# A delta-rule and soft-MoE kernel: the instruction order of its attention part written by hand instead of by the scheduler

## The chip, the cores and the metric

The kernel runs on one core of one Trainium2 chip. The metric is device microseconds of one execution. A core has TensorE (PE, with its weight loads shown apart as PEld), VectorE (DVE), ScalarE (ACT), GpSimd (POOL) and the DMA queue of SyncE (SP). Each engine runs its own instructions in the order in which they were emitted; engines wait for each other by semaphores.

## The reference

A delta-rule attention runs over 768 tokens for 4 batches of 8 heads with 48 numbers a head; its output, as 3072 rows of 384, goes through a soft mixture of experts with 8 experts of 4 slots.

```python
k_n = k / (np.linalg.norm(k, axis=-1, keepdims=True) + 1e-06)
for t in range(S):
    y[:, :, t] = q_t @ state
    state += beta_t * outer(k_t, v_t - k_t @ state)
logits = x @ phi
d = softmax(logits, axis=0); slot_input = d.T @ x
slot_out[e] = relu(slot_input[e] @ w1[e]) @ w2[e]
out = softmax(logits, axis=1) @ slot_out
```

## The kernel before

The attention is cut into 24 chunks of 32 tokens, numbered 0 to 23 (`x` or `cc` in the code), and six groups of four chunks (`n`; `c` is the place of a chunk in its group, 0 to 3). All 32 heads are worked on together. The state of a chunk is the next chunk's input, so the chunks make one chain. A chunk's chain (function `chunk`) has these links, in this order:

- psR: 16 products of the old state with the keys on PE (L278, into psR), and as many with the queries (into psY)
- R: values minus psR, on DVE (L283)
- psW: 32 small products of R with the inverse of the group (TT) on PE (L289), copied to U by ACT (L292)
- psS: 32 products that update the state on PE (L299), copied out by ACT for one half (L311) and then by DVE for the other (L309), both called S
- outputs: 32 products into psY (L316), copied to Y by ACT (L318). They are not needed by the next chunk.

Beside the chain runs work for later and earlier chunks:

- Preparation (`prep`) of the chunk eight places ahead: two times four transposes of K and Q (L173, copied to KQ by ACT, L176), then 32 products (L188), whose two halves ACT copies to Lc (L194) and DVE to AT (L195). The PSUM tile pt, of which there are two, serves all of this and the routing.
- The inverse (`invert`) of the next group, mainly on DVE: `spread` (L207) and `norms` (L221 to L233, with one square root on ACT, L222), a scaling on POOL (lb, L230), then 31 steps of an elimination, each a product (pr, L240) and a subtraction (tt, L243) that follow each other, then a scaling on POOL (L247) and a transpose into TT (L253). The group's first solve needs TT.
- Scaling of V two chunks ahead on POOL (L259).
- Routing (`route`) of the group that was finished last: four turns of Y (L336), logits (L345), a transpose to lg (L351, L352), softmax over slots (L356 to L364), a running maximum (L370 to L385), weights d (L389), a repeat of d by PE (L398), and four slot products (L410) added to sacc on DVE.

Loads of K and Q run twelve chunks ahead on the SP queue, loads of V six.

What sets the order: the Python code emits a chunk's chain with calls of `fill()` in three places and at the end, and each call emits a share of a merged list of preparation, inverse and routing steps. The scheduler of the framework then orders the instructions of each engine by its own estimates; the code's order is only one of its inputs. Chunks -8 to -1 emit preparation and the first inverse alone. After chunk 23 the last routing is drained, the attention's memory is given up, the weights of the remaining experts are loaded, and the experts and the output run (L489 to L600). That last part is called the tail here.

Of the kernel before, what the change touches and what calls it, by code (L numbers as in the profile page):

```python
# [16 lines left out]
def kernel(  # L17
# [23 lines left out]
    nc = tc.nc  # L41
# [225 lines left out]
    def chunk(cc, Yn, fill):  # L267
# [5 lines left out]
        pr = ps.tile([P, B, G, D], F32, name="psR", tag="psRW")  # L273
        py = ps.tile([P, B, G, D], F32, name="psY", tag="psY")
        for a, dst in enumerate((pr, py)):
# [5 lines left out]
            if a == 0:  # L281
                R = wk.tile([P, U, D], F32, name="R", tag="R")
                nc.vector.tensor_tensor(R, Vt.pop(cc), pr.rearrange("p b g d -> p (b g) d"),  # L283
                                        op=ALU.subtract)
        fill()
        pw = ps.tile([P, U, D], F32, name="psW", tag="psRW")
        for u in range(U):
            for h in range(4):
                nc.tensor.matmul(pw[hs[h], u], lhsT=T[hs[h], u], rhs=R[hs[h], u],  # L289
                                 start=(u == 0), stop=True, skip_group_check=True)  # L290
        Ut = wk.tile([P, U, D], F32, name="U", tag="U")
        nc.scalar.activation(Ut, pw, ACT.Copy)  # L292
        fill()

        if cc < NCH - 1:
            for b in range(B):
                for g in range(G):
                    for h in range(4):
                        nc.tensor.matmul(psS[DP * g:DP * g + D, h, b * D:(b + 1) * D],  # L299
                                         lhsT=K[hs[h], b * G + g, 0:D],  # L300
                                         rhs=Ut[hs[h], b * G + g],
# [10 lines left out]
            fill()  # L312
        for b in range(B):
            for g in range(G):
                for h in range(4):
                    nc.tensor.matmul(py[hs[h], b, g], lhsT=at[hs[h], g, b], rhs=Ut[hs[h], b * G + g],  # L316
                                     start=False, stop=True, skip_group_check=True)
        nc.scalar.activation(Yn[:, c, :, 0:GD], py.rearrange("p b g d -> p b (g d)"), ACT.Copy)  # L318
# [7 lines left out]
    def route(n, Yn):  # L326
# [13 lines left out]
        def logits():  # L340
# [7 lines left out]
            lT = wk.tile([P, P], F32, name="lT", tag="lT", bufs=1)  # L348
            nc.scalar.activation(lT, pl, ACT.Copy)
            pq = pt([P, P])  # L350
            nc.tensor.transpose(pq, lT, ident)  # L351
            nc.vector.tensor_copy(lg.rearrange("p b s -> p (b s)"), pq)  # L352

        def over_slots():
            mx = small.tile([P, B], F32, name="mx", tag="mx")
            nc.vector.tensor_reduce(mx, lg, axis=AX.X, op=ALU.max)  # L356
            el = small.tile([P, B, NSL], F32, name="el", tag="el")
            nc.vector.tensor_tensor(el, lg, mx.unsqueeze(2).broadcast_to([P, B, NSL]),
                                    op=ALU.subtract)
            nc.scalar.activation(el, el, ACT.Exp)  # L360
            nc.vector.tensor_reduce(mx, el, axis=AX.X, op=ALU.add)
            nc.vector.tensor_scalar(mx, mx, 1e-9, None, op0=ALU.add)
            nc.vector.reciprocal(mx, mx)
            nc.gpsimd.tensor_tensor(Call[:, n], el, mx.unsqueeze(2).broadcast_to([P, B, NSL]),  # L364
                                    op=ALU.mult)

        def maximum():

            cm = small.tile([P, 4, NSL], F32, name="cm", tag="cm")
# [3 lines left out]
                                  cm[:, 0, :].unsqueeze(1).broadcast_to([P, 3, NSL]))  # L373
            pm = pt([P, P])
# [3 lines left out]
            else:  # L378
# [6 lines left out]
                nc.vector.tensor_copy(mrun, m1)  # L385
            pmb = pt([P, NSL])
# [33 lines left out]
        return ([lambda b=b: turn(b) for b in range(B)] + [logits, over_slots, maximum, repeat]  # L420
# [7 lines left out]
    NF = 4  # L428

    class Fill:  # L430


        def __init__(self, steps):
            self.steps, self.at, self.calls = steps, 0, 0

        def __call__(self, last=False):
            self.calls += 1
            to = len(self.steps) if last else len(self.steps) * min(self.calls, NF) // NF
            while self.at < to:
                self.at += 1  # L440
                self.steps[self.at - 1]()

    def merge(*lists):

        keyed = [((i + 0.5) / len(ls), j, f) for j, ls in enumerate(lists) for i, f in enumerate(ls)]
        return [f for _, _, f in sorted(keyed, key=lambda x: x[:2])]

# [5 lines left out]
    def quarter(ls, c):  # L453
        return ls[len(ls) * c // GC:len(ls) * (c + 1) // GC]

    routing, inv = [], []
    for x in range(-LEAD, NCH):
# [6 lines left out]
        if 1 <= n + 2 and x == -4:  # L464
            for e in range(NW1):
                load_w1(e, wpool, NW1)
        if c == 0:
            inv = invert(n + 1) if 0 <= n + 1 < NG else []
# [4 lines left out]
        if x < 0:  # L473
# [155 lines left out]
```

## Time and profile before

| what | us |
|---|---|
| median of 3 runs | 491.54 |
| lowest, highest | 484.33, 493.37 |
| the profiled execution, whole | 491.42 |
| its span, first to last instruction | 489.7 |

The span is the time that all rows below count in; the profiled execution is 1.72 us longer than it. A row of the timeline names a start, a duration, an engine, a line, an operation, the tile written, the tiles read, and in brackets how long the engine had been idle and who ended that. A row of the chain names a start, a duration and a piece of work that the end waited for. A row of the waits names the waiting engine, tile and line, whom it waited for, the sum, the count and the longest. A row of the windows gives, for a stretch, the busy time of each engine with its number of instructions, and the mean clock granted to TensorE (1.00 is 2.4 GHz, 0.50 is 1.2 GHz).

### The profile page before, as it was taken

The numbers are of one execution on the slowest core, as the hardware profiler recorded it, in microseconds if no ns is written. First come the engines' busy times: TensorE is split into PE (matmuls) and PEld (weight loads), VectorE is DVE, ScalarE is ACT, GpSimd is POOL, SyncE is SP. The second block draws the span as 40 slices with busy tenths as digits, with TensorE's granted clock in tenths as the row PEclk, the third lists the DMA queues.
The fourth block names the chain that finished last, engine by engine and source line by source line (L and its number), as shares of the span: only waits on it lengthen the run. The fifth ranks groups of instructions, "written<-read, shape, count | busy, mean of one in ns | idle before, by whom it ended". The sixth has DMA issues, their size and how long they took to land.

```text
span 489.7 us, 20564 instructions
## 1 busy us (share of the span) xinstructions
PE 334.7 (68%) x9387; PEld 248.3 (51%) x9387; DVE 245.1 (50%) x679; ACT 128.9 (26%) x257; POOL 63.6 (13%) x88
## 2 busy tenths in 40 slices
PE   5743374656766758788677776876875865788586
PEld 4532263545645646666466655665664753532133
DVE  4159716972168942379721788325997212210033
ACT  2331122121322422332422233224312222111012
POOL 9210112012020040020210200202301000000000
PEclk9655556665766759755778577599798797799695
DMA  6557742320322213202221110010300029949427
GB/s 114 86 94 195 205 83 51 52 37 18 52 51 39 46 19 52 50 16 40 51 39 33 19 19 13 9 20 5 113 23 1 4 94 367 424 156 434 208 101 287
DMA packets 84759, 45.53 MB, mean 93 GB/s; under 512 B 79392, under 2 KB 82624, under 8 KB 82624
## 3 DMA queue, kind: packets, MB, share of 16 engines
q1 hardware_dynamic: 81920, 43.67, 32.4%
q8 instruction: 74, 1.21, 1.0%
q10 hardware_dynamic: 2176, 0.39, 0.4%
q0 software_dynamic: 576, 0.15, 0.3%
q14 instruction: 13, 0.11, 0.1%
HBM read 39.47 MB, written 4.72 MB: 90 GB/s over the span
## 4 chain that ended last, share of the span: by engine, by line
DVE 27%; issue 25%; PE 19%; SPq 10%; DMA 10%; POOL 5%; ACT 3%; DVEq 0%; POOLq 0%; ACTq 0%
DVE pr L240 9%; SPq L80 9%; DVE tt L243 9%; DMA w2t<-in_moe_w_dram 4%; PE pso L567 3%; DVE S L309 3%; PE psR L278 2%; PE pt L410 2%; DMA w1t<-in_moe_w_dram 2%; PE psY L278 2%; POOL lb L230 2%; DMA Q<-in_q_dram 2%; DVE TT L253 2%; PE ph L543 1%; DMA out_dram<-ob 1%
## 5 line engine op out<-in xcount | busy, mean ns | idle before, releaser
L240 DVE TENSOR_TENSOR pr<-tt,lb 128x31 f32<-128x31 f32 (+15 forms) x186 | 68.0, 365 | 17.7 <-POOL lb L230 12.2
L243 DVE TENSOR_TENSOR tt<-tt,pr 128x31 f32<-128x31 f32 (+15 forms) x186 | 66.3, 357 | 5.7
L289 PE MATMUL psW<-R,TT 32*32 32x48 f32 x1536 | 29.9, 242 | 47.0 <-DVE R L283 45.5
L173 PE MATMUL pt<-ident,K 128*128 128x128 f32 x96 | 36.0, 396 | 24.1 <-DVE AT L195 18.7
L289 PEld LDWEIGHTS psW<-R,TT 32*32 32x32 f32 x1536 | 25.7, 134 | 52.4 <-DVE R L283 49.3
L176 ACT ACTIVATE KQ<-pt 128x512 f32<-128x512 f32 x48 | 27.1, 595 | 73.9 <-PE pt L173 73.5
L278 PE MATMUL psR<-S,KQ 128*32 128x96 f32 x768 | 33.1, 324 | 17.7 <-DVE S L309 17.0
L316 PE MATMUL psY<-U,AT 32*32 32x48 f32 x1536 | 39.0, 256 | 3.2 <-issue 3.1
L195 DVE TENSOR_TENSOR AT<-pt,tri 128x128 f32<-128x128 f32 x48 | 11.9, 288 | 54.6 <-ACT Lc L194 54.4
L188 PE MATMUL pt<-KQ 48*32 48x64 f32 x1536 | 33.5, 246 | 6.2 <-ACT KQ L176 2.6
L309 DVE COPY S<-psS 48x768 f32<-48x768 f32 x23 | 22.1, 961 | 31.1 <-ACT S L311 30.7
L316 PEld LDWEIGHTS psY<-U,AT 32*32 32x32 f32 x1536 | 31.1, 143 | 9.2 <-issue 7.1
L299 PE MATMUL psS<-U,K 32*48 32x48 f32 x1472 | 25.3, 261 | 14.5 <-ACT U L292 11.6
L278 PEld LDWEIGHTS psR<-S,KQ 128*32 128x32 f32 x768 | 23.7, 145 | 22.4 <-DVE S L309 18.9
L188 PEld LDWEIGHTS pt<-KQ 48*32 48x32 f32 x1536 | 25.0, 119 | 16.0 <-ACT KQ L176 9.5
L173 PEld LDWEIGHTS pt<-ident,K 128*128 128x128 f32 x96 | 17.3, 186 | 30.7 <-DVE AT L195 20.2
L278 PE MATMUL psY<-S,KQ 128*32 128x96 f32 x768 | 32.3, 314 | 0.0
L292 ACT ACTIVATE U<-psW 128x384 f32<-128x384 f32 x24 | 11.8, 490 | 75.6 <-PE psW L289 75.6
L299 PEld LDWEIGHTS psS<-U,K 32*48 32x48 f32 x1472 | 20.4, 155 | 20.7 <-ACT U L292 15.7
L410 PE MATMUL pt<-Y,dr 32*32 32x97 f32 x768 | 25.1, 271 | 8.5 <-DVE AT L195 4.3
L230 POOL TENSOR_TENSOR lb<-lb,gm 128x1024 f32<-128x1024 f32 x6 | 11.5, 1911 | 141.0 <-DVE gm L229 141.0
L173 PE MATMUL pt<-ident,Q 128*128 128x128 f32 x96 | 29.7, 364 | 0.0
(124 smaller groups left out, 454.9 us busy)
## 6 DMA issues: line engine op xcount, KB each, us to landing
w1t<-in_moe_w_dram SPq DMA_DIRECT2D x8, 1536.0 KB, 8.2
w2t<-in_moe_w_dram SPq DMA_DIRECT2D x8, 1536.0 KB, 15.1
K<-in_k_dram SPq DMA_DIRECT2D x96, 48.0 KB, 2.3
V<-in_v_dram SPq DMA_DIRECT2D x96, 48.0 KB, 2.3
out_dram<-ob SPq DMA_DIRECT2D x24, 192.0 KB, 2.3
Q<-in_q_dram SPq DMA_DIRECT2D x88, 48.0 KB, 2.3
Q<-in_q_dram ACTq DMA_DIRECT2D x8, 48.0 KB, 3.0
bb<-in_beta_dram POOLq DMA_DIRECT2D x16, 6.0 KB, 3.0
```

What stands on the lines that cost most here:

```text
L80: eng.dma_start(out=dst[C * h:C * h + C, :, 0:D], in_=src.rearrange("b (g h) s d -> h s (b g) d", h=4)[h, cc * C:(cc + 1) * C])
L173: nc.tensor.transpose(tp[:, i, a, :], src[:, b * G:(b + 1) * G, :].rearrange("p g d -> p (g d)"), ident)
L176: nc.scalar.activation(KQ[cc][:, 2 * bh:2 * bh + 2], tp, ACT.Copy)
L188: nc.tensor.matmul(pg[g][rh, b], lhsT=KQ[cc][r, b, 0, rh], rhs=KQ[cc][r, b, :, rh], start=True, stop=True, skip_group_check=True)
L240: nc.vector.tensor_tensor(prv, tt[:, j, 0:m].unsqueeze(1).broadcast_to([P, w, m]), lb[:, j, j + 1:C].unsqueeze(2).broadcast_to([P, w, m]), ...
L243: nc.vector.tensor_tensor(tt[:, j + 1:C, 0:m], tt[:, j + 1:C, 0:m], prv, op=ALU.subtract)
L278: nc.tensor.matmul(dst[hs[h], b].rearrange("p g d -> p (g d)"), lhsT=kq[:, b, a, hs[h]], rhs=old[:, h, b, :], start=(b == 0), stop=False, ...
L289: nc.tensor.matmul(pw[hs[h], u], lhsT=T[hs[h], u], rhs=R[hs[h], u], start=(u == 0), stop=True, skip_group_check=True)
L299: nc.tensor.matmul(psS[DP * g:DP * g + D, h, b * D:(b + 1) * D], lhsT=K[hs[h], b * G + g, 0:D], rhs=Ut[hs[h], b * G + g], start=(cc == 0 a ...
L309: nc.vector.tensor_copy(dst, src)
L316: nc.tensor.matmul(py[hs[h], b, g], lhsT=at[hs[h], g, b], rhs=Ut[hs[h], b * G + g], start=False, stop=True, skip_group_check=True)
L410: nc.tensor.matmul(pa[r], lhsT=st["dr"][r, c, b, :], rhs=Yn[r, c, b, 0:GD + 1], start=(b == 0), stop=(b == B - 1), skip_group_check=True)
```

## The change

The attention part is emitted inside `tc.manual_schedule()`, where each engine gets its instructions in the order of the code. `chunk` now returns its five links as functions, the routing's steps are cut so that each holds one pass from one engine to the next (logits and by_tokens, maxima, over_tokens, shares, weights), and `plan` deals the 31 elimination steps of a group over five places in each of its four chunks. The arithmetic, the tiles, the buffers and the loads are the same. The last routing's drain and the tail stand outside of the hand order.

```diff
-    def chunk(cc, Yn, fill):
+    def chunk(cc, Yn):
...
+        return rest, read, solve, update, outputs
...
-        return ([lambda b=b: turn(b) for b in range(B)] + [logits, over_slots, maximum, repeat]
+        return ([lambda b=b: turn(b) for b in range(B)]
+                + [logits, by_tokens, maxima, over_tokens, shares, weights, repeat]
                 + [lambda c=c: slots(c) for c in range(GC)])
...
+    PLACES = 5
+    cost = [2 * (160 + (j + 1) * (C - 1 - j)) for j in range(C - 1)]
+    share = [(0.0, 0.0, 0.05, 0.05, 0.07), (0.05, 0.06, 0.06, 0.06, 0.07),
+             (0.05, 0.06, 0.06, 0.06, 0.07), (0.08, 0.08, 0.07, 0.0, 0.0)]
...
+        at[0][0] += [spread, norms]
...
+        at[GC - 1][2] += el[i:] + [scale]
+        at[GC - 1][4] += [back]
...
+    order = tc.manual_schedule()
+    order.__enter__()
...
-        steps = merge(prep(x + LEAD) if x + LEAD < NCH else [], quarter(inv, c),
-                      quarter(routing, c))
...
-        fill = Fill(steps)
-        chunk(x, Ys[n % 2], fill)
-        fill(last=True)
...
+        def place(p):
+            if EL:
+                drain(EL[c][p])
+            i, j = len(rt) * p // PLACES, len(rt) * (p + 1) // PLACES
+            drain(rt[i:j])
+
+        x0, x1, xp = prep(x + LEAD) if x + LEAD < NCH else [lambda: None] * 3
...
+        rest()
         if 0 <= x + 2 < NCH:
             scale_v(x + 2)
...
+        read()
+        x0()
+        place(0)
+        solve()
+        x1()
+        place(1)
+        update()
+        outputs()
+        place(2)
+        xp()
+        place(3)
+        place(4)
...
+    order.__exit__(None, None, None)
     drain(routing)
```

In this text place 0 to place 4 are those of `place(p)`: places 0 and 1 stand on DVE between R and the S copy of the same chunk, places 2 to 4 between that S copy and the next chunk's R. By the 15 routing steps of a group, chunk 0 has a turn in places 1, 3 and 4; chunk 1 the last turn, logits, by_tokens and maxima in places 1 to 4; chunk 2 over_tokens, shares, weights and repeat in places 1 to 4; chunk 3 a slot product in each of places 1 to 4.

On DVE, the stretch behind an R in the second group of the main loop, before (AT is preparation, L240 and L243 are the elimination, L283 is R):

```order
L195 TENSOR_TENSOR AT<-pt,tri 128x128 x2
L243 TENSOR_TENSOR tt<-tt,pr 128x18x14
L240 TENSOR_TENSOR pr<-tt,lb 128x255
L243 TENSOR_TENSOR tt<-tt,pr 128x17x15
L283 TENSOR_TENSOR R<-V,psR 128x384
L240 TENSOR_TENSOR pr<-tt,lb 128x256
L243 TENSOR_TENSOR tt<-tt,pr 128x16x16
```

and now (L286 is R, L318 the S copy):

```order
L286 TENSOR_TENSOR R<-V,psR 128x384
L240 TENSOR_TENSOR pr<-tt,lb 128x192
L243 TENSOR_TENSOR tt<-tt,pr 128x24x8
L240 TENSOR_TENSOR pr<-tt,lb 128x207
L243 TENSOR_TENSOR tt<-tt,pr 128x23x9
L240 TENSOR_TENSOR pr<-tt,lb 128x220
L243 TENSOR_TENSOR tt<-tt,pr 128x22x10
L318 COPY S_180<-psS 48x16x48
L240 TENSOR_TENSOR pr<-tt,lb 128x231
L243 TENSOR_TENSOR tt<-tt,pr 128x21x11
L195 TENSOR_TENSOR AT<-pt,tri 128x128 x2
```

Before, eleven rows of the elimination stand between that R and the S copy behind it, and the 62 rows of a whole elimination in the main loop contain one R and two S copies (the first two groups), two and two (the next two) or three and three (the last). Now six rows stand there, and every elimination of the main loop is spread over its four chunks, with three R and three S copies among its rows. In the lead-in the first elimination contained two pairs of AT products; now it contains three, and a fourth stands ahead of TT.

On PE, the same chunk 5 from its solve on, before (L289 solve, L299 update, L316 outputs, L173 transposes of preparation, L336 a routing turn):

```order
L289 MATMUL psW<-R,TT 32x48 x32
L299 MATMUL psS<-U,K_81 48x48 x30
L173 MATMUL pt<-ident,K_88 128x128
L336 MATMUL pt<-ident,Y_187 96x128 x4
L299 MATMUL psS<-U,K_81 48x48 x2
L316 MATMUL psY<-U,AT 32x48 x17
```

and now (L297 solve, L350 a turn, L308 update, L326 outputs, L359 logits, L188 products of preparation):

```order
L297 MATMUL psW<-R,TT 32x48 x32
L173 MATMUL pt<-ident,K_76 128x128
L173 MATMUL pt<-ident,Q_92 128x128
L173 MATMUL pt<-ident,K_76 128x128
L173 MATMUL pt<-ident,Q_92 128x128
L350 MATMUL pt<-ident,Y_187 96x128 x4
L308 MATMUL psS<-U,K_81 48x48 x32
L326 MATMUL psY<-U,AT 32x48 x32
L359 MATMUL pt<-yT,phi 32x128 x16
L188 MATMUL pt<-KQ 32x64 x32
```

Before, single transposes and a turn cut the update in two. Now half of the preparation's transposes and the turn stand ahead of the update, in the time in which ACT makes U, and the update is whole.

On POOL, the first group's inverse and the first two V, before:

```order
L247 TENSOR_TENSOR tt<-tt,gm 128x1024
L211 MEMSET tt 128x1024
L212 MEMSET tt 128x32
L259 TENSOR_TENSOR V<-V,nT 128x384 x2
```

and now:

```order
L259 TENSOR_TENSOR V<-V,nT 128x384 x2
L247 TENSOR_TENSOR tt<-tt,gm 128x1024
L259 TENSOR_TENSOR V<-V,nT 128x384
L211 MEMSET tt 128x1024
```

The first two V now stand ahead of the last scaling of the inverse instead of behind two memsets that follow it.

## Rows read from the trace of the kernel before

**Rows 1.** The page, busy time of each engine, share of the span, instructions.

```profile
PE 334.7 (68%) x9387; PEld 248.3 (51%) x9387; DVE 245.1 (50%) x679; ACT 128.9 (26%) x257; POOL 63.6 (13%) x88
```

**Rows 2.** The lines of R (L283) and TT (L253): instructions, first and last start.

```profile
L283 DVE TENSOR_TENSOR R<-V,psR x24: 495/552/555, 62.9 to 399.0; 128x384 f32<-128x384 f32 x24
...
L253 DVE STREAM_TRANSPOSE TT<-tt x6: 1902/1918/1945, 58.9 to 374.1; 128x1024 f32<-128x1024 f32 x6
```

**Rows 3.** Windows: first R to that of chunk 20, to the last R, to the end.

```profile
62.90:366.40 303.50, 218.58 (x7193) 175.28 (x7193) 178.48 (x487) 90.13 (x175) 40.93 (x42) 0.72 0.20 38
366.40:399.00 32.60, 23.09 (x901) 18.92 (x904) 14.77 (x39) 9.17 (x18) 2.31 (x2) 0.84 0.01 4
399.00:489.70 90.70, 65.12 (x739) 32.71 (x727) 16.79 (x45) 14.59 (x33) 0.84 (x4) 0.80 0.71 279
```

**Rows 4.** Waits: who waited for whom, us in total, times, longest.

```profile
DVE AT L195 <- ACT Lc L194: 54.4, 15, 7.3
...
PE psW L289 <- DVE R L283: 45.5, 15, 10.1
```

**Rows 5.** Timeline of DVE over one whole inverse, 137 to 176 us.

```profile
136.99 1.23 DVE L207 STREAM_TRANSPOSE lb<-Lc 128x1024 f32<-128x1024 f32 x1
...
140.69 0.19 DVE L229 TENSOR_TENSOR gm<-gm,bb 128x32 f32<-128x32 f32 x1
142.91 0.80 DVE L240 TENSOR_TENSOR pr<-tt,lb 128x31 f32<-128x31 f32 x1 [2.02 <-POOL lb L230]
...
155.56 0.51 DVE L195 TENSOR_TENSOR AT<-pt,tri 128x128 f32<-128x128 f32 x2 [1.22 <-ACT Lc L194]
...
170.10 0.29 DVE L352 COPY lg<-pt 128x128 f32<-128x128 f32 x1
...
171.27 0.20 DVE L240 TENSOR_TENSOR pr<-tt,lb 128x31 f32<-128x31 f32 x1
171.50 0.19 DVE L243 TENSOR_TENSOR tt<-tt,pr 128x31 f32<-128x31 f32 x1
173.72 1.92 DVE L253 STREAM_TRANSPOSE TT<-tt 128x1024 f32<-128x1024 f32 x1 [2.02 <-POOL tt L247]
```

**Rows 6.** The chain that ended last, in order of time, from the R of chunk 20 on.

```profile
366.43 0.55 DVE R L283
...
376.10 1.54 PE psW L289 x64
...
383.41 1.01 PE psW L289 x63
...
384.50 0.50 ACT U L292
...
385.04 0.83 PE psS L299 x51
...
395.29 0.81 ACT S L311
396.13 0.97 DVE S L309
...
398.18 0.74 PE psR L278 x25
```

**Rows 7.** The chain again: a routing repeat, a slot product, a turn, the logits.

```profile
316.45 1.33 PE pt L398 x32
...
332.16 0.87 PE pt L410 x32
...
404.37 0.58 PE pt L336 x4
...
409.42 2.41 PE pt L345 x32
```

**Rows 8.** Timeline of POOL and DVE at 209 us.

```profile
209.58 1.61 POOL L259 TENSOR_TENSOR V<-V,nT 128x384 f32<-128x384 f32 x2
...
209.65 0.80 DVE L240 TENSOR_TENSOR pr<-tt,lb 128x31 f32<-128x31 f32 x1 [2.03 <-POOL lb L230]
```

More of the change, by code (lines that the diff above doesn't have):

```diff
@@ L272, in chunk, with state @@
         hs = [slice(C * h, C * h + C) for h in range(4)]
-        pr = ps.tile([P, B, G, D], F32, name="psR", tag="psRW")
-        py = ps.tile([P, B, G, D], F32, name="psY", tag="psY")
-        for a, dst in enumerate((pr, py)):
+        st = {}
+        def state(a, dst):
             for b in range(B):
@@ L280, in chunk, with rest, read, solve @@
                                      start=(b == 0), stop=False, skip_group_check=True)
[L281 to L295, printed above, removed]
+        def rest():
+            pr = ps.tile([P, B, G, D], F32, name="psR", tag="psRW")
+            state(0, pr)
+            R = st["R"] = wk.tile([P, U, D], F32, name="R", tag="R")
+            nc.vector.tensor_tensor(R, Vt.pop(cc), pr.rearrange("p b g d -> p (b g) d"),
+                                    op=ALU.subtract)
+        def read():
+            st["py"] = ps.tile([P, B, G, D], F32, name="psY", tag="psY")
+            state(1, st["py"])
+        def solve():
+            pw = ps.tile([P, U, D], F32, name="psW", tag="psRW")
+            for u in range(U):
+                for h in range(4):
+                    nc.tensor.matmul(pw[hs[h], u], lhsT=T[hs[h], u], rhs=st["R"][hs[h], u],
+                                     start=(u == 0), stop=True, skip_group_check=True)
+            st["U"] = wk.tile([P, U, D], F32, name="U", tag="U")
+            nc.scalar.activation(st["U"], pw, ACT.Copy)
+        def update():
+            if cc == NCH - 1:
+                return
             for b in range(B):
@@ L300, in chunk @@
                                          lhsT=K[hs[h], b * G + g, 0:D],
-                                         rhs=Ut[hs[h], b * G + g],
+                                         rhs=st["U"][hs[h], b * G + g],
                                          start=(cc == 0 and b == 0), stop=True,
@@ L426, in drain @@
                 f()
[L428 to L446, printed above, removed]
     Ys = [wk.tile([P, GC, B, GD + 4], F32, name=f"Y{i}", bufs=1) for i in range(2)]
@@ L451, with plan @@
         nc.gpsimd.memset(t[:, :, :, GD:GD + 4], 1.0)
-    def quarter(ls, c):
-        return ls[len(ls) * c // GC:len(ls) * (c + 1) // GC]
-    routing, inv = [], []
+    EL = {}
+    PLACES = 5
+    cost = [2 * (160 + (j + 1) * (C - 1 - j)) for j in range(C - 1)]
+    share = [(0.0, 0.0, 0.05, 0.05, 0.07), (0.05, 0.06, 0.06, 0.06, 0.07),
+             (0.05, 0.06, 0.06, 0.06, 0.07), (0.08, 0.08, 0.07, 0.0, 0.0)]
+    def plan(n):
+        spread, norms, *el, scale, back = invert(n)
+        at = [[[] for _ in range(PLACES)] for _ in range(GC)]
+        at[0][0] += [spread, norms]
+        flat = [(c, p) for c in range(GC) for p in range(PLACES)]
+        i, done, total = 0, 0.0, 0.0
+        for c, p in flat:
+            total += share[c][p]
+            while i < len(el) and (done + cost[i] / 2) / sum(cost) < total:
+                done += cost[i]
+                at[c][p].append(el[i])
+                i += 1
+        at[GC - 1][2] += el[i:] + [scale]
+        at[GC - 1][4] += [back]
+        return at
+    order = tc.manual_schedule()
+    order.__enter__()
+    routing = []
     for x in range(-LEAD, NCH):
```

67 lines of the change are left out of this document (37 added, 30 removed).

## Prediction

> **What bounds the kernel now.** I read the busy times first, then windows by stage, the waits, one whole inverse on DVE, and last the chain that ended last. No engine is full: PE is busy 68% of the span, DVE 50% [rows 1]. The first R starts at 62.9 us and the last at 399.0 [rows 2], which cuts the span into a lead-in of 62.9, the groups with an inverse beside them (chunks 0 to 19, 303.5 us, 60.7 a group), chunks 20 to 22 (32.6) and the tail (90.7) [rows 3]. In the 303.5 us DVE is busy for 178.5 with 487 instructions [rows 3], so 125 us are idle or hand-over, though DVE carries the inverse on which the next group's first solve waits. The reader is to see why in the timeline of one inverse [rows 5]: its 62 elimination rows run from 142.91 to 171.69 nearly without a break, and the front's excerpt of the order shows one R and two S copies among them. A chunk's R that came due in that block waits for its row. PE's solve waits 45.5 us in 15 pieces for R, up to 10.1 us each [rows 4]. Then the block is over, and DVE has too little to do until the next one: it waits 54.4 us for ACT in front of AT [rows 4]. So the kernel alternates between a DVE bound and a bound by the chain, and pays for both one after the other. The change spreads the block over the four chunks.
>
> **The sum, part by part.** Durations are of the profiled execution: 491.42 us, span 489.70, so 1.72 lie outside of the span; the median of the runs, 491.54, is nearly the same.
>
> *Lead-in.* R of chunk 0 starts at 62.9 though TT begins at 58.9 and takes 1.92 [rows 2, 5]; in POOL's order of before the first two V stand behind the memsets that follow TT. Now V is ready long before. Against it two more pairs of AT products stand ahead of TT, 0.5 each [rows 5]: 58.9 + 1.9 + 1.0 + 0.1 = 61.9.
>
> *One chunk's chain from R to the end of its S copy.* R 0.55, psW 1.01, U 0.50, psS 0.83, the S copies 0.81 and 0.97 [rows 6], and six hand-overs of about 0.05 (from the gaps between these rows): 5.0 us. The S copy of DVE starts at 4.0.
>
> *The elimination.* Its 62 rows span 28.8 us [rows 5], of which the order puts into the stretch two S copies (1.9), an R (0.5), an AT pair with its wait (1.7) and five routing pieces (0.6, interleaved): 24 us are left. The shares give chunk 0 4.1 us behind its S copy; chunks 1 and 2 2.6 ahead of it and 4.6 behind; chunk 3 3.9 ahead and 1.7 behind. Ahead of the S copy there are 4.0 − 0.5 = 3.5 us that DVE has to wait anyhow, so 2.6 is hidden fully and 3.9 nearly. What stands behind it is on the path: the next R is queued behind it on DVE.
>
> *Chunk 0.* Spread and norms take 3.9 us to the end of gm, with an R of 0.4 among them [rows 5]: 3.5, hidden as above. But U on ACT now stands behind the square root, which needs DVE's spread; I put 0.9 for that and 0.5 for the turn ahead of psS [rows 7]. Behind S: 4.1 and AT 0.5. 5.0 + 0.9 + 0.5 + 4.6 = 11.0.
> *Chunk 1.* 5.0, a turn 0.5, elimination 4.6, AT 0.5. The logits stand ahead of preparation's products on PE; they took 2.41 at the slow clock [rows 7], I put 1.3 of delay of AT. Five routing pieces at about 0.3 (the copy to lg took 0.29) [rows 5]: 1.5. Sum 13.4.
> *Chunk 2.* The running maximum stands on DVE and ACT ahead of the S copies: 5.0 + 1.0. Behind S a round trip stands on PE ahead of the next psR: shares 0.6, elimination 2.8, AT 0.5, d 0.3, its exponential 0.35, the repeat 1.33 [rows 7], psR 1.1 (0.74 and the few products ahead of it) [rows 6]. Sum 13.0.
> *Chunk 3.* 5.0, a slot product ahead of psS 0.9 [rows 7], elimination 1.7, POOL's scaling 2.0, TT 1.9 [rows 5], sacc 0.3: 11.8.
> That is 49.2 a group with routing. Without routing (group 0) the chunks come to 10.5, 10.1, 10.1 and 10.6: 41.3.
>
> *V beside the elimination.* With two V scalings on POOL from 209.58 on, the first pr takes 0.80 us; the same shape takes 0.20 at 171.27, where none ran [rows 5, 8]. Three of a group's four V now stand beside elimination rows. My price is 0.6 for one, and two of them are new or were not in the 24 us: 1.2 a group. The lower bound is 0 (they fall into waits of DVE), the upper 3 × 0.8 = 2.4.
> By the Trainium skill (SBUF — State Buffer, section SBUF: two separate sides) a DVE instruction with two SBUF inputs and a GpSimd one share a port pair that is an exclusive lock: whoever starts first holds it for its whole instruction. Here the trace agrees, 0.80 against 0.20. The rule speaks against this change, since it spreads two-input rows over the whole group: by it every V, four of 0.8 us, would hold one up, 3.2 a group, and the sum below would be 10 us higher.
>
> *Groups in all.* 41.3 + 4 × 49.2 + 5 × 1.2 = 244.1, against 303.5.
>
> *Chunks 20 to 22.* No elimination and no preparation, but routing: 5.0 + psR 1.1 + 0.6 for a turn = 6.7; 5.0 + 0.5 + logits, lT and the transpose 1.6 + 1.1 = 8.2; 6.0 + d, exponential and repeat 2.0 + 1.1 + 0.4 = 9.5. Together 24.4 against 32.6, in which before waited for the last elimination and TT (R of chunk 20 at 366.43, its psW at 376.10) [rows 6].
>
> *Tail.* The drain of the last routing and the expert part are the same code outside of the hand order, and the loads of weights wait for tiles that the last chunks give up, so it moves as a whole: 90.7.
>
> 61.9 + 244.1 + 24.4 + 90.7 = 421.1, and 1.7 outside: 423 us, 68 less than before.
>
> What is not shown by any row: a clock other than the one granted. Most of my PE durations are from a stretch with 0.84, while the groups had 0.72 [rows 3]. psW took 1.54 at 376.10 and 1.01 at 383.41 [rows 6]. If PE stands closer together the clock should rise, so I take the short ones; with the long ones each of psW, psS, psR and preparation's products adds up to 0.5, 2 us a chunk, 40 in all. In the other direction, DVE's own work allows 178.5 + 487 × 0.04 = 198 us for the five groups instead of 244.
>
> **Rivals.**
> A. DVE fills up almost without waits, since my stalls (AT 1.3, the round trip in chunk 2, the root in chunk 0) fall beside each other. For it: 198 us of DVE work for 303.5 now. Against it: every chunk has three places where DVE waits for a single release. At 43 us a group: 61.9 + 215 + 24.4 + 90.7 + 1.7 = 394.
> B. TensorE becomes the bound: preparation, routing and chain in one order on one engine at the low clock. For it: 0.72 now, and three link products at 1.0 to 1.5 us each. 423 + 40 = 463. It decides when PE is never idle ahead of psR.
> C. Slower. The one-hop pieces of routing each stand in PE's and DVE's order ahead of a chain step, and each waits for a release that itself stands behind a DVE portion (a pt tile that AT frees, a transpose that needs the copy behind elimination rows). If every one of the 15 steps of the four groups with routing cost a whole portion, 0.06 × 24 = 1.5 us, beyond what is counted, that is 60 × 1.5 = 90: 513. It is slower than before from 1.15 us a step on. Against it: only seven of the 15 stand between preparation's products and the next psR on PE.
> D. The hand order does not do what it says: R and S still stand behind blocks as long as before, and the 45.5 us of PE's wait for R come back in places 2 to 4. Then 303.5 stays and only the lead-in is won: 490. Against it: the order itself, six rows in place of eleven and no run over 10 rows.
>
> **How the numbers follow.** My sum 0.62, A 0.17, B 0.13, C 0.05, D 0.03. The prediction is that of the likeliest, 423. The range 390 to 458 takes in most of A's spread and the nearer part of B and leaves out the far part of B, C, D and A's best case, some 0.2. A change can be told from none here from about 2%, 10 us. The sum, A and B are all faster by more: 0.92; within 2% D: 0.03; slower C: 0.05.
>
> **What would show it.** R to R about 10 us in group 0 and 11 to 13.5 after it; the 62 elimination rows spread over some 40 us instead of 29; PE's wait for R under 20 us in all; DVE busy over 70% from the first to the twenty-first R; the first R at about 62; the tail 90 us long. The prediction is wrong if groups take over 57 us (then the waits of PE tell B from C: no idle time in B, releases by DVE in C), if the tail grows because a weight load comes later, or if the clock falls under 0.7.

## The result and the profile after

The changed kernel takes 438.39 us (median of 4 runs, 435.23 to 442.24), the kernel before 489.31 in the same session (4 runs, 484.33 to 493.37): a ratio of 0.897, with a 95% interval of 0.884 to 0.910. The profiled execution took 437.39 us, with a span of 435.7. A later session gave 438.54 (434.6 to 441.22) for the same kernel, ratio 0.893 (0.886 to 0.901). The forecast was 423 with 390 to 458: the right side and inside of the range, 15 us too low. Runs more than 1.5% above a kernel's fastest are left out of the ratios, but not of the medians.

The page of the changed kernel, busy times, against [rows 1]:

```profile
PE 299.1 (69%) x9387; PEld 227.6 (52%) x9387; DVE 248.9 (57%) x679; ACT 129.1 (30%) x257; POOL 63.5 (15%) x88
```

The instructions are the same in number, and DVE's work is nearly the same (248.9 for 245.1 us). PE's busy time fell from 334.7 to 299.1.

The lines of R (now L286) and TT, first and last start, against [rows 2]:

```profile
L286 DVE TENSOR_TENSOR R<-V,psR x24: 522/552/556, 64.5 to 348.2; 128x384 f32<-128x384 f32 x24
L253 DVE STREAM_TRANSPOSE TT<-tt x6: 1939/1945/2014, 62.7 to 320.3; 128x1024 f32<-128x1024 f32 x6
```

Windows of the changed kernel from the first R to that of chunk 20, on to the last R, and to the end, against [rows 3]:

```profile
64.50:322.30 257.80, 182.22 (x7116) 152.45 (x7116) 187.52 (x503) 87.63 (x170) 42.25 (x44) 0.82 0.24 45
322.30:348.20 25.90, 20.53 (x828) 17.20 (x832) 7.60 (x20) 9.30 (x18) 0.40 (x1) 0.84 0.01 4
348.20:435.70 87.50, 64.58 (x807) 33.48 (x799) 17.18 (x47) 14.61 (x33) 0.84 (x4) 0.85 0.73 289
```

| stage, us | before | forecast | after | after, second profile |
|---|---|---|---|---|
| lead-in, to the first R | 62.9 | 61.9 | 64.5 | 64.6 |
| group 0 | 62.8 | 42.5 | 44.7 | 46.1 |
| group 1 | 62.3 | 50.4 | 52.4 | 54.9 |
| group 2 | 67.2 | 50.4 | 55.4 | 54.8 |
| group 3 | 64.9 | 50.4 | 57.3 | 55.6 |
| group 4 | 46.4 | 50.4 | 48.0 | 47.5 |
| chunks 20 to 22 | 32.6 | 24.4 | 25.9 | 26.3 |
| tail | 90.7 | 90.7 | 87.5 | 88.6 |

(A group is the time from the R of its first chunk to the R of the next group's.) The last column is the later session's profile of the same kernel: single groups differ by up to 2.5 us between the two, the five together by 1.1, so smaller differences in one group are not read as effects below. The five groups gave back 45.7 us, chunks 20 to 22 6.7 and the tail 3.2; the lead-in lost 1.6. DVE is busy for 187.52 of the 257.8 us, 73% against 59%: its idle time there fell from 125.0 us to 70.3. PE's idle time fell only from 84.9 to 75.6; the larger part of the gain stands in its busy time, 182.22 us for 218.58 with nearly the same matmuls, while the granted clock of TensorE over the groups rose from 0.72 to 0.82.

Waits of the changed kernel, against [rows 4] (waiting engine, tile and line, whom it waited for, sum, times, longest):

```profile
DVE S L318 <- ACT S L320: 31.4, 22, 3.9
PE psW L297 <- DVE R L286: 28.0, 11, 4.1
DVE AT L195 <- ACT Lc L194: 24.7, 13, 4.1
PE pt L173 <- DVE AT L195: 21.0, 9, 4.4
```

PE's wait for R went from 45.5 us, up to 10.1 each, to 28.0, up to 4.1 each; DVE's wait in front of AT from 54.4 to 24.7. The other two sums were there before, in fewer and longer pieces:

```profile
DVE S L309 <- ACT S L311: 30.7, 10, 4.4
PE pt L173 <- DVE AT L195: 18.7, 6, 8.9
```

DVE's wait for ACT's half of S is a wait on the chain itself, now in 22 of 23 chunks; in the other PE waits for AT to free a pt tile.

### The profile page after: what moved, and what is told of

Same layout as the page of the kernel before. It is cut to its first block, busy times and chain, and to the rows that moved or that the text cites. A ratio compares the mean times of both kernels' runs of the same rounds, so it can differ in the third digit from the quotient of the medians.

```text
span 435.7 us, 20600 instructions
## 1 busy us (share of the span) xinstructions
PE 299.1 (69%) x9387; PEld 227.6 (52%) x9387; DVE 248.9 (57%) x679; ACT 129.1 (30%) x257; POOL 63.5 (15%) x88
## 5 line engine op out<-in xcount | busy, mean ns | idle before, releaser
L240 DVE TENSOR_TENSOR pr<-tt,lb 128x31 f32<-128x31 f32 (+15 forms) x186 | 68.5, 368 | 9.5 <-POOL lb L230 4.7
L243 DVE TENSOR_TENSOR tt<-tt,pr 128x31 f32<-128x31 f32 (+15 forms) x186 | 68.2, 367 | 6.4
L173 PE MATMUL pt<-ident,K 128*128 128x128 f32 x96 | 34.3, 371 | 26.6 <-DVE AT L195 21.0
L297 PE MATMUL psW<-R,TT 32*32 32x48 f32 x1536 | 25.8, 224 | 28.6 <-DVE R L286 28.0
L297 PEld LDWEIGHTS psW<-R,TT 32*32 32x32 f32 x1536 | 22.1, 122 | 34.4 <-DVE R L286 31.4
L318 DVE COPY S<-psS 48x768 f32<-48x768 f32 x23 | 22.1, 960 | 31.4 <-ACT S L320 31.4
L188 PE MATMUL pt<-KQ 48*32 48x64 f32 x1536 | 30.7, 263 | 11.9 <-issue 5.5
L173 PEld LDWEIGHTS pt<-ident,K 128*128 128x128 f32 x96 | 17.0, 178 | 32.7 <-DVE AT L195 23.3
L173 PE MATMUL pt<-ident,Q 128*128 128x128 f32 x96 | 32.2, 348 | 0.9 <-issue 0.9
L188 PEld LDWEIGHTS pt<-KQ 48*32 48x32 f32 x1536 | 21.9, 125 | 20.4 <-ACT KQ L176 8.7
L326 PE MATMUL psY<-U,AT 32*32 32x48 f32 x1536 | 26.4, 219 | 5.4 <-issue 5.3
L278 PE MATMUL psY<-S,KQ 128*32 128x96 f32 x768 | 28.8, 306 | 1.1 <-issue 1.1
L278 PE MATMUL psR<-S,KQ 128*32 128x96 f32 x768 | 29.4, 310 | 0.2
L431 PE MATMUL pt<-Y,dr 32*32 32x97 f32 x768 | 24.4, 278 | 6.7 <-issue 3.5
L247 POOL TENSOR_TENSOR tt<-tt,gm 128x1024 f32<-128x1024 f32 x6 | 11.5, 1912 | 103.0 <-DVE tt L243 89.9
L195 DVE TENSOR_TENSOR AT<-pt,tri 128x128 f32<-128x128 f32 x48 | 12.0, 289 | 25.0 <-ACT Lc L194 24.7
L326 PEld LDWEIGHTS psY<-U,AT 32*32 32x32 f32 x1536 | 21.8, 117 | 8.1 <-issue 6.4
L278 PEld LDWEIGHTS psY<-S,KQ 128*32 128x32 f32 x768 | 24.9, 144 | 1.5 <-issue 1.3
L431 PEld LDWEIGHTS pt<-Y,dr 32*32 32x32 f32 x768 | 20.6, 123 | 9.1 <-issue 4.6
L194 ACT ACTIVATE Lc<-pt 128x128 f32<-128x128 f32 x48 | 14.6, 405 | 33.2 <-PE pt L188 33.2
```

The source lines that it names most:

```text
L173: nc.tensor.transpose(tp[:, i, a, :], src[:, b * G:(b + 1) * G, :].rearrange("p g d -> p (g d)"), ident)
L188: nc.tensor.matmul(pg[g][rh, b], lhsT=KQ[cc][r, b, 0, rh], rhs=KQ[cc][r, b, :, rh], start=True, stop=True, skip_group_check=True)
L194: nc.scalar.activation(by[:, c, g], pg[g][:, :, 0, :], ACT.Copy)
L240: nc.vector.tensor_tensor(prv, tt[:, j, 0:m].unsqueeze(1).broadcast_to([P, w, m]), lb[:, j, j + 1:C].unsqueeze(2).broadcast_to([P, w, m]), ...
L243: nc.vector.tensor_tensor(tt[:, j + 1:C, 0:m], tt[:, j + 1:C, 0:m], prv, op=ALU.subtract)
L297: nc.tensor.matmul(pw[hs[h], u], lhsT=T[hs[h], u], rhs=st["R"][hs[h], u], start=(u == 0), stop=True, skip_group_check=True)
```

## The experiments

The theory to test: what the kernel before lost was the place of the elimination on DVE, so spreading the rows is the gain. Rivals: the finer routing, or the order on PE, is the gain, or the scheduler is to blame whatever the code says. Ratios are to the kernel before, run in the same session.

**The scheduler back, on the new code.**

```diff
-    order = tc.manual_schedule()
-    order.__enter__()
...
-    order.__exit__(None, None, None)
```

> The changed code with its cut pieces and its dealing of the elimination, but ordered by the scheduler again. Theory (the gain comes from the order on DVE: elimination rows no longer stand in one block in front of R and S): the scheduler gathers the block again, 475 to 500 us, and PE waits 35 us or more for R. Rival 1 (the finer routing pieces alone are the gain): 430 to 450 us. Rival 2 (half and half): 455 to 470 us.

Measured 477.63 us, ratio 0.978 (0.971 to 0.985). The five groups took 62.4, 60.4, 61.0, 61.4 and 50.3, 295.5 together for 303.5 before. The waits of this kernel:

```profile
PE psW L297 <- DVE R L286: 33.7, 14, 10.1
```

The wait for R has again pieces of 10.1 us, and each elimination of the main loop spans 27 to 33 us with one to three R among its rows, as before. The new cut of the steps alone brings some 10 us (7 to 14 by the interval); the rest needs the order.

**The old code in the order in which it is written.** The kernel before, with its even spread and its coarse routing, inside `tc.manual_schedule()` up to the drain of the last routing.

> The code of before, with its fill calls and its coarse routing, but emitted in the hand order. Its elimination is dealt evenly over four chunks too. Theory (spreading on DVE is nearly all of the gain): 435 to 455 us, group 0 within 2 us of the 44.7 of the changed kernel. Rival (the chain-first cut, the shares and the one-hop pieces are the gain): 470 to 495 us.

Measured 450.43 us, ratio 0.921 (0.914 to 0.929): 38 of the 50 us come with no new cut at all. The groups took 44.4, 55.0, 56.1, 59.2 and 52.2. The waits of this kernel:

```profile
DVE S L309 <- ACT S L311: 25.2, 18, 4.4
DVE AT L195 <- ACT Lc L194: 15.5, 9, 4.1
PE psW L289 <- DVE R L283: 12.6, 9, 2.8
```

PE waits less for R than in the changed kernel (12.6 for 28.0), but in groups 1 to 4 the S copy of chunks 0 and 2 ends 9 to 12 us after R, where the changed kernel has 5 to 7: here four to ten elimination rows and, in chunk 2, the whole maximum stand between R and S, where the changed kernel has none to six.

**The whole elimination in one block.** All 31 steps behind the S copy of chunk 0:

```diff
-    share = [(0.0, 0.0, 0.05, 0.05, 0.07), (0.05, 0.06, 0.06, 0.06, 0.07),
-             (0.05, 0.06, 0.06, 0.06, 0.07), (0.08, 0.08, 0.07, 0.0, 0.0)]
+    share = [(0.0, 0.0, 1.01, 0.0, 0.0)] + [(0.0,) * 5] * 3
```

> The changed kernel, with all 31 elimination steps of a group in one block behind the S copy of the group's first chunk. Theory: the block of 24 us stands on the path; what was hidden ahead of the S copies (2 x 2.6 + 3.9 = 9 us a group) is lost and the other chunks become shorter by their 15 us, so plus 9 a group, 45 in all: 475 to 490 us. Rival (the whole order of PE is what counts): 435 to 450 us.

Measured 530.99 us, ratio 1.088 (1.081 to 1.095). The direction was expected, the size was not. The five groups took 336.7 us for 257.8, and the first R came 11.3 us later. The timeline of DVE and that of PE around the block of group 1 (between the first two rows DVE waits 0.69 us for POOL's scaling and then runs the 62 rows without a break):

```profile
142.82 0.96 DVE L318 COPY S<-psS 48x768 f32<-48x768 f32 x1 [0.26 <-ACT S L320]
...
169.00 0.49 DVE L195 TENSOR_TENSOR AT<-pt,tri 128x128 f32<-128x128 f32 x2
172.79 0.55 DVE L286 TENSOR_TENSOR R<-V,psR 128x384 f32<-128x384 f32 x1 [3.31 <-PE psR L278]
```

```profile
143.73 0.86 PE L188 MATMUL pt<-KQ 48*32 48x64 f32 x64
169.34 1.94 PE L350 MATMUL pt<-ident,Y 128*96 128x128 f32 x8 [24.75 <-DVE AT L195]
171.22 1.51 PE L278 MATMUL psR<-S,KQ 128*32 128x96 f32 x32
```

PE stands 24.75 us for AT, which frees the pt tile for a turn, and psR of the next chunk is queued behind the turn. The first chunk of a group took 31 to 35 us. But the other three got little shorter for having no elimination: by 1.3, 3.1, 5.5, 7.9 and 8.6 us together in groups 0 to 4, 5.2 a group, though the changed kernel has some 17.8 of a group's 22.9 us of elimination rows there. So in the changed kernel most of these rows cost nothing where they stand.

**The old cut of the routing.** The function `route` of before (four longer steps in place of seven) in the changed kernel.

> The changed kernel with the routing's old coarse steps (12 instead of 15; logits with the transpose to lg, the whole softmax over slots, the whole maximum with d). Theory (routing pieces matter only where PE waits for a round trip ahead of psR): the maximum's two round trips on PE stand ahead of one chain step, plus 2 to 5 us a group with routing, 448 to 460 us. Rival 1 (one-hop pieces are the main gain): 470 us or more. Rival 2 (no matter): 434 to 443 us.

Measured 447.88 us, ratio 0.915 (0.907 to 0.922), just under the expected range and some 10 us over the changed kernel. The S copy of chunk 2 ends 9.3 to 10.0 us after R in place of about 6: there the longer step stands between R and S. But the theory expected 2 to 5 us a group, and the five groups took only 1.4 more (259.2): chunk 2 got 1 to 3 us longer in groups 1 to 4, and chunk 3 of groups 2 and 3 about as much shorter. The rest stands in chunks 20 to 22 (29.2 for 25.9) and in the tail (92.7 for 87.5).

**Without the elimination.** `el = []` in `plan`.

> The changed kernel without the 62 elimination instructions of every group (the inverse is left out of the computation). By my sum 15 us a group stand on the path behind the S copies: minus 75 us in the five groups, about 360 us. By the theory that the run with the elimination in one block suggests (its chunks without elimination took 11.4 to 13 us, hardly less than with it): most of the elimination hides beside PE and the chain, minus 4 to 8 us a group and some 24 us in the lead-in: 375 to 395 us.

Measured 394.84 us (two runs, 391.48 and 398.2). The lead-in is 15.1 us shorter (24 expected), the five groups together 32.1 (225.7 for 257.8): 6.4 a group, where the forecast had put 15 a group on the path. PE's busy time in the groups is 6.9 us lower too, at a granted clock of 0.86 for 0.82, so a part of the 6.4 may be PE's. The waits of this kernel:

```profile
DVE S L318 <- ACT S L320: 58.9, 23, 7.0
DVE AT L195 <- ACT Lc L194: 56.2, 21, 5.1
```

Against 31.4 and 24.7 in the changed kernel, DVE waits 27.5 us more in front of S and 31.5 more in front of AT, of which 26.5 and 19.2 in the five groups and 12.3 in the lead-in. So that much of the elimination lay in waits that come anyway: both ahead of the S copy, as forecast, and behind it, which the forecast had put on the path. The gain is uneven: 0.7, 1.9, 7.9, 9.0 and 12.7 us in groups 0 to 4. The first two are not a clean price, since with the lead-in 15 us shorter V arrives late (POOL waits 26.2 us for its loads in group 0). Group 4, where no preparation runs and so no wait for AT exists, pays most.

**Without the routing** of groups 1 to 5, in the main loop and in the last drain; the first group's, which runs beside group 1, stays.

> The changed kernel with the routing of group 0 alone; that of groups 1 to 5 is left out, in the loop and in the drain at the end. If routing is what makes groups 2 and 3 take 55 and 57 us instead of 45: groups 2 and 3 at 44 to 46 us, group 4 (no preparation) below 42, the last R at 305 to 318 us instead of 348, and a tail shorter by the 15 to 20 us of the last drain. If the chip's clock or the queues make later groups long: groups 2 and 3 stay over 50 us.

Measured 400.19 us (two runs, 399.27 and 401.11), ratio 0.823 (0.815 to 0.830). Groups 2 and 3 took 47.1 and 45.4 for 55.4 and 57.3, 8.3 and 11.9 less; group 4 42.6, 5.4 less; chunks 20 to 22 22.0, 3.9 less. So in groups 2 and 3 the routing costs the chain as much as the elimination or more (7.9 and 9.0 there), and the clock is not what makes them long: over the groups it was 0.78 here, under the 0.82 of the changed kernel. Three of the expected numbers were missed: group 4 is not below 42, the last R comes at 320.7 instead of 305 to 318, and the tail is 8.9 us shorter (78.6) instead of 15 to 20.

**Without the scaling of V.**

> The changed kernel without the scaling of V on POOL (left out of the computation). By the lock rule of the Trainium skill's page on SBUF, every scaling holds up an elimination instruction by its whole 0.8 us: 3.2 us a group, minus 16 us. By the rows of the changed kernel (three of four stand beside elimination rows, 0.5 to 0.6 each): minus 8 us. If the elimination is mostly hidden: minus 0 to 4 us, within the noise.

Measured 427.72 us (426.74 to 432.82), ratio 0.881 (0.874 to 0.889). The groups took 248.3 us together, 9.5 less, 1.9 a group, over the spread of 1.1 between the two profiles of the changed kernel. The forecast had 1.2.

**The routing steps at other places.** The turns stay where they were; the logits and their transpose stand behind preparation's products in chunk 1, the steps after them a place or more later, the repeat and the slot products late in chunk 3, through a table:

```diff
-            i, j = len(rt) * p // PLACES, len(rt) * (p + 1) // PLACES
-            drain(rt[i:j])
+            if routing:
+                drain([routing[i] for i in AT_PLACE.get((c, p), [])])
...
+    AT_PLACE = {(0, 1): [0], (0, 3): [1], (0, 4): [2], (1, 1): [3], (1, 3): [4], (1, 4): [5],
+                (2, 0): [6], (2, 2): [7, 8], (2, 3): [9], (3, 2): [10], (3, 3): [11, 12], (3, 4): [13, 14]}
```

> The changed kernel with the routing steps at other places, so that no round trip stands ahead of psR and none ahead of preparation's products: logits behind the products, maxima in place 0 of chunk 2, the running maximum behind chunk 2's outputs, the repeat behind chunk 3's outputs. Theory (round trips of routing on PE ahead of chain steps cost 3 to 4 us a group): minus 8 to 18 us, 420 to 430 us. Rival (PE's own work is the bound, wherever it stands): 434 to 442 us.

Measured 440.59 us (436.09 to 443.45), ratio 0.903 (0.895 to 0.911): no gain, in the range of the rival. The groups gave 8.0 us (249.8 together), but chunks 20 to 22 took 28.2 (25.9 in the changed kernel) and the tail 94.9 (87.5): in chunk 23 the late repeat and four slot products stand on PE behind the outputs, ahead of the last routing.

**The same for chunks 4 to 19 only.**

> The other places of the routing steps (turns in places 1, 3, 4 and 1; logits behind preparation's products; slot products behind TT's chunk's products) for chunks 4 to 19 alone, and the changed kernel's own places in chunks 20 to 23, where the routing stands ahead of the drain. Theory (what the groups gained in the run with the places moved throughout was given back in the last four chunks and the drain): groups 1 to 3 about 156 us together instead of 165, chunks 20 to 22 at 26.0 and the tail at 87.5 as in the changed kernel, so some 430 us. Rival (the gain in the groups only moves idle time, a later stage takes it): 438 as before, with chunks 20 to 22 or the tail longer again.

Measured 437.54 us (433.76 to 440.94), ratio 0.891 (0.884 to 0.898), against 438.54 and 0.893 (0.886 to 0.901) for the changed kernel in the same session: not to be told apart, as the rival had it. The groups took 251.9 in this profile against 258.9 in that session's profile of the changed kernel, so 7.0 us were won there; chunk 1 of groups 1 to 3 went from 12.8, 13.6 and 13.8 to 11.5, 11.7 and 11.0. Chunks 20 to 22 took 1.5 more, and the tail 90.0 for 88.6. Its two parts, from the last R to the last slot product and from there to the end, first of this kernel, then of the changed one in its first profile:

```profile
344.30:370.20 25.90, 18.46 (x498) 14.88 (x488) 4.88 (x21) 4.94 (x11) 0.84 (x4) 0.71 0.91 360
370.20:434.30 64.10, 48.46 (x311) 19.08 (x307) 12.26 (x26) 9.78 (x22) 0.00 (x0) 0.87 0.63 249
```

```profile
348.20:371.70 23.50, 17.61 (x500) 14.41 (x492) 4.92 (x21) 4.83 (x11) 0.84 (x4) 0.81 0.86 337
371.70:435.70 64.00, 46.97 (x309) 19.07 (x307) 12.26 (x26) 9.78 (x22) 0.00 (x0) 0.87 0.68 271
```

The expert part is 64 us in both (64.8 in the second profile). The last routing's drain is a chain of its own: 25.9 us here at a granted clock of 0.71, 23.5 at 0.81 and 23.8 at 0.77 in the two profiles of the changed kernel. The last run below, which has the same routing places, took 25.3 at 0.77, so the clock alone does not explain it; what does is not shown.

**Norms behind the solve, TT ahead of the slot sums.** On top of the last run:

```diff
-        at[0][0] += [spread, norms]
+        at[0][0] += [spread]
+        at[0][1] += [norms]
...
-        at[GC - 1][4] += [back]
+        at[GC - 1][3] += [back]
```

> The same, and the norms with their square root emitted behind the chunk's solve instead of ahead of it, and TT ahead of the slot products' sums on DVE instead of behind them. Theory (the head of a group pays for ACT's order, U behind the square root, and its end for TT behind sacc): U follows psW in chunk 0 (1 to 2 us a group less) and TT starts as soon as POOL's scaling ends (1 to 2 us a group less): 10 us under the run before it, some 420. Rival (DVE has other work there and the start of the elimination only moves): within 3 us of the run before it.

Measured 452.19 us (445.32 to 456.17), ratio 0.914 (0.905 to 0.922): slower than the run before it, against the theory. The two moves were made together; the next run, which has them too, shows where each of them costs.

**V where no elimination runs.** On top of that:

```diff
-        if 0 <= x + 2 < NCH:
-            scale_v(x + 2)
+        if c == 0 and x >= 0:
+            scale_v(x + 2)
+            scale_v(x + 3)
...
         xp()
+        if c == GC - 1 and 0 <= x + 1 < NCH:
+            scale_v(x + 1)
+            scale_v(x + 2)
```

> The same as the last, and the four scalings of V of a group put where no elimination row runs: two behind POOL's last scaling in chunk 3, two at the head of chunk 0. Theory (V costs 1.9 us a group, as the run without V showed, because it runs beside two-input rows of the elimination): some 8 us under the run before it. Rival (on a path at POOL they delay the lb scaling and the memsets): no gain or a loss of up to 4 us, 0.8 a group.

Measured 442.49 us (438.99 to 444.71), ratio 0.904 (0.896 to 0.911). By the ratios that is 5 us less than the run before it, and the two intervals overlap, so the expected 8 us are not shown. All six first pr rows took 0.19 us, as none did in the changed kernel, and the elimination's 372 rows 127.2 us for 136.7; the kernel as a whole did not get faster than the changed one for it. The timeline of DVE at the end of chunk 19 (after the elimination's last row at 311.29) and of PE beside it:

```profile
313.57 1.93 DVE L253 STREAM_TRANSPOSE TT<-tt 128x1024 f32<-128x1024 f32 x1 [2.09 <-POOL tt L247]
315.53 0.32 DVE L436 SCALAR_TENSOR_TENSOR sacc<-sacc,al,pt 128x97 f32<-128x97 f32 x1
...
320.28 0.55 DVE L286 TENSOR_TENSOR R<-V,psR 128x384 f32<-128x384 f32 x1 [1.24 <-PE psR L278]
```

```profile
315.91 2.81 PE L431 MATMUL pt<-Y,dr 32*32 32x97 f32 x64 [3.36 <-DVE sacc L436]
318.65 1.51 PE L278 MATMUL psR<-S,KQ 128*32 128x96 f32 x32
```

With TT ahead of the sums, the sums wait 2.09 for POOL and 1.93 for TT; they free the two pt tiles, so PE's next slot products wait 3.36, and psR stands behind them. Chunk 19 took 15.3 us for 11.3 (10.8 in the second profile); chunks 7, 11 and 15, which have the same order but preparation beside it, show no such loss against the run with the places moved for chunks 4 to 19. The norms: in this run DVE waits 3.46 us for the square root in chunk 8, and S stands behind the norms:

```profile
167.58 0.35 DVE L223 RECIPROCAL rn<-nrm 128x32 f32<-128x32 f32 x1 [3.46 <-ACT nrm L222]
...
169.60 0.96 DVE L318 COPY S<-psS 48x768 f32<-48x768 f32 x1
```

The end of S came 8.4 us after R there, against 6.1 and 7.0 in the two profiles of the changed kernel. The delay went from U on ACT to S on DVE. No version that computes everything came out measurably better than the changed kernel.

## Why the prediction was right, and where it was 15 us short

**Mechanism: right in its main step.** The kernel before lost time around one long block on DVE, and the order is what removes it: with the scheduler back 40 of the 50 us are gone, and with the block put back by hand, at one place for all rows, the kernel is slower than before. Rival D (the order doesn't do what it says) falls by the waits for R and by the groups, rival C (slower) by the result; A and B are 44 us under and 25 over the measured time. The rows of the elimination spread over 34.5 to 43.2 us in the main loop (forecast 40), DVE is busy 73% (over 70%). Not all signs came: the chunks of groups 1 to 3 took 13.1 to 14.3 us on the mean (11 to 13.5 forecast), and group 3, with 57.3 in one profile and 55.6 in the other, touched the 57 us that the forecast had named as a sign of being wrong.

The two kinds of gain are not separated by any run. Of the 45.7 us of the groups, 9.3 are idle time of PE and 36.4 its busy time. The forecast allowed for that: it took PE's short durations, which it put at 40 us in all against the long ones. In the kernel before, the time does not follow the clock from run to run: in one session it took 488.9 us at a mean granted clock of 0.73 and 486.71 at 0.81. Open as well is the share of each engine's order: the block shows what the places on DVE are worth with the order on PE unchanged, but no run has the new order on one engine and the scheduler's on the other.

**The step that failed: "What stands behind it is on the path".** The forecast put the elimination behind the S copies in series with the chain, 15 us a group by the shares and 13.2 in the sums of the chunks, and counted psR behind S in chunk 2 alone. Taken out, the elimination gives 6.4 a group. What the next R waits for stands in the rows of S, psR and R. psR in the pages of the two kernels, before and now (busy time, mean, and idle time of PE ahead of it):

```profile
L278 PE MATMUL psR<-S,KQ 128*32 128x96 f32 x768 | 33.1, 324 | 17.7 <-DVE S L309 17.0
```

```profile
L278 PE MATMUL psR<-S,KQ 128*32 128x96 f32 x768 | 29.4, 310 | 0.2
```

One passage from chunk to chunk of the kernel before, DVE, then PE:

```profile
147.45 0.96 DVE L309 COPY S<-psS 48x768 f32<-48x768 f32 x1
...
157.24 0.55 DVE L283 TENSOR_TENSOR R<-V,psR 128x384 f32<-128x384 f32 x1
```

```profile
148.46 1.51 PE L278 MATMUL psR<-S,KQ 128*32 128x96 f32 x32 [1.97 <-DVE S L309]
```

Before, psR started as soon as S was there, and R stood behind the block: over the twelve passages behind chunks 4 to 15, psR starts 0.5 us after the end of S on the mean, and R 6.6 us after the end of psR. In the changed kernel psR starts 5.1 us after S and R 1.1 after psR. Without the elimination the two are 4.5 and 0.1. So what the chain waits for behind S is now mostly PE's row: outputs, preparation's products and routing stand ahead of psR, some of them waiting for DVE themselves. That is the sign that the forecast had for rival B, PE never idle ahead of psR, though PE is idle elsewhere for 75.6 of the 257.8 us. The forecast's step holds where R still comes late after psR: in group 0 (2.9 to 4.9 us), ahead of the R of chunks 6, 10 and 14 (3.6) and of chunks 17 and 18 (4.1 and 3.1). The sum had an elimination term that was too large and no term for PE's row. The two errors cancel in part, most in group 1 and least in group 3; that the total came as near as 15 us is so far luck.

**Where the 15 us lie: behind the S copy, and in chunk 3 above all.** By chunk, the mean of groups 1 to 3 against the forecast: 12.6 for 11.0, 13.9 for 13.4, 14.2 for 13.0, 14.4 for 11.8 (V's 1.2 a group aside). Of these nearly 6 us a group 4.5 lie between the end of S and the next R. The sum had 7.9 us a group for routing; removing it gave 8.3, 11.9 and 5.4 in groups 2 to 4. Without routing these groups took 47.1, 45.4 and 42.6, where the sum has 42.5, so what was undersized is the group without routing as well as the routing of group 3. Chunk 3 of group 3 shows how routing delays the chain there, first PE, then DVE, then POOL:

```profile
266.75 0.53 PE L431 MATMUL pt<-Y,dr 32*32 32x97 f32 x15 [1.17 <-issue]
...
268.15 1.04 PE L188 MATMUL pt<-KQ 48*32 48x64 f32 x62 [0.63 <-DVE sacc L439]
269.98 2.81 PE L431 MATMUL pt<-Y,dr 32*32 32x97 f32 x64 [0.79 <-DVE AT L195]
272.71 1.51 PE L278 MATMUL psR<-S,KQ 128*32 128x96 f32 x32
```

```profile
265.31 0.96 DVE L318 COPY S<-psS 48x768 f32<-48x768 f32 x1 [1.31 <-ACT S L320]
...
267.83 0.26 DVE L439 TENSOR_TENSOR sacc<-sacc,pt 128x97 f32<-128x97 f32 x1
269.63 0.51 DVE L195 TENSOR_TENSOR AT<-pt,tri 128x128 f32<-128x128 f32 x2 [1.54 <-ACT Lc L194]
271.56 0.26 DVE L439 TENSOR_TENSOR sacc<-sacc,pt 128x97 f32<-128x97 f32 x1 [1.42 <-PE pt L431]
271.73 1.94 DVE L253 STREAM_TRANSPOSE TT<-tt 128x1024 f32<-128x1024 f32 x1
...
274.29 0.55 DVE L286 TENSOR_TENSOR R<-V,psR 128x384 f32<-128x384 f32 x1 [0.53 <-PE psR L278]
```

```profile
267.95 1.91 POOL L247 TENSOR_TENSOR tt<-tt,gm 128x1024 f32<-128x1024 f32 x1 [14.42 <-DVE tt L243]
```

A slot product stands on PE ahead of preparation's products, whose pt tile needs the sum on DVE; so AT is late (1.54), the next slot products wait for AT (0.79), the next sum waits for them (1.42), and TT, ready from 269.86 on by POOL, starts at 271.73 behind that sum. The chain itself gets the delay through PE: S ends at 266.27, psR starts at 272.71 behind the slot products, and R waits for it (0.53). The forecast had elimination, scaling and TT in a row and sacc at 0.3. Chunk 1 has the same form: the logits ahead of the products make AT wait 2.41 us at 239.37 (forecast 1.3); the run with the places moved for chunks 4 to 19 has them behind, and that chunk took 1.3 to 2.8 us less.

**Missed: group 4 has no preparation.** Preparation runs eight chunks ahead and ends with chunk 15, so from chunk 16 on there is no AT. Group 4 took 48.0, not 50.4.

**Lead-in: wrong sign.** TT starts at 62.7, not at 58.9, so R at 64.5 for 61.9 (62.9 before). The square root on ACT stands behind its table load of 1.28, DVE waits 1.79 us for it, the first elimination row starts at 35.3 (32.9 before) and takes 0.80 beside V, which in the kernel before was not scaled until later. The gain from V standing ahead of TT was taken by what V and ACT's order cost earlier; without the scaling of V the first R stands at 63.3.

**V: mechanism right, size 1.2 for 1.9 a group.** The timeline of POOL and DVE at the head of group 4 in the changed kernel, and then in the run with V moved (DVE rows of group 2; V's four scalings were done at 159.03 there):

```profile
280.33 1.62 POOL L259 TENSOR_TENSOR V<-V,nT 128x384 f32<-128x384 f32 x2
...
280.41 0.80 DVE L240 TENSOR_TENSOR pr<-tt,lb 128x31 f32<-128x31 f32 x1 [0.76 <-POOL lb L230]
281.24 0.78 DVE L243 TENSOR_TENSOR tt<-tt,pr 128x31 f32<-128x31 f32 x1
```

```profile
155.84 3.19 POOL L259 TENSOR_TENSOR V<-V,nT 128x384 f32<-128x384 f32 x4
...
171.47 0.19 DVE L240 TENSOR_TENSOR pr<-tt,lb 128x31 f32<-128x31 f32 x1 [0.91 <-POOL lb L230]
171.69 0.21 DVE L243 TENSOR_TENSOR tt<-tt,pr 128x31 f32<-128x31 f32 x1
```

Two rows of one pair lose 0.6 each to two V, and 9.5 us (136.7 less 127.2) of DVE's rows go over six eliminations. By the rule of the Trainium skill (SBUF — State Buffer, section SBUF: two separate sides), of a GpSimd instruction that reads SBUF and a DVE instruction with two SBUF inputs the one that starts first holds the shared ports for its whole length and the other waits. The 0.80 beside V and the 0.19 without it agree; taken as a price the rule gave 3.2 a group, and 1.9 was measured. That the rest falls on rows or waits off the chain is a reading; no run shows it.

**PE's clock and waits.** Taking PE's durations at a higher clock was right: the granted clock over the groups rose from 0.72 to 0.82. PE's wait for R, forecast under 20, is 28.0. Of it 10.8 stand ahead of the solves of chunks 0 to 4, 8.6 ahead of those of chunks 6, 10 and 14, whose R stands on DVE behind elimination rows and the five routing pieces that follow a late AT, and 7.1 in chunks 17 and 18.

**Chunks 20 to 22 and the tail.** 25.9 for 24.4, and 87.5 for 90.7: the drain and the loads did move as a whole.

## What to carry to other kernels

When one engine carries both a long side job and a short link of the chain, deal the side job out in portions no longer than the waits that come anyway; whether a portion is free is seen by removing it, not by adding up the order. In a hand order each step that frees a shared tile (here the two pt tiles) is a link of the chain for everything queued behind the step that wants the tile: put the work that frees the tile early, and look on both engines before moving a step, since a delay taken from one queue (U behind the square root) came back in another (S behind the norms). And look at the end of a loop when work moves later inside it: the 8 us won in the groups by the places moved throughout were paid there, and of the 7 us won with the end unmoved the medians show 1, which is within the noise.

## What was not expected of the hardware

PE's busy time fell by 35.6 us (334.7 to 299.1) with the same 9387 matmuls, while the granted clock over the groups rose from 0.72 to 0.82: a gain counted in waits alone misses that. The mean clock of a stretch does not give the busy time, though. With the elimination in one block PE was busy for 174.8 us over the five groups at a mean clock of 0.75, less than in the changed kernel at 0.82 (182.2), with nearly the same matmuls (7108 and 7116): the mean counts PE's idle stretches too. And the effect of V on DVE, read from two rows ahead of the forecast, was found throughout: a V scaling of 0.8 us on POOL stretched the first row of the elimination from 0.19 us to 0.80 in five of the six inverses before and in all six after the change, and with V left out or moved away all six took 0.19.
